# Products of the key/value stage on ScalarE, weight conversions behind the last scores, and other banks for `rp` and the first `vp`, in an attention and MoE kernel

## The chip, the cores and the metric

The kernel runs on one core of a Trainium2 chip. The metric is the device time of one execution in microseconds (us). A core has TensorE (PE, its weight load PEld), VectorE (DVE), ScalarE (ACT), GpSimd (POOL) and SyncE (SP, which here only issues DMAs). PSUM, the memory that TensorE writes, is handed out in banks; SBUF holds everything else on the chip.

## The reference, cut to what matters

```
a   = softmax(phi, over the 576 positions)            # phi (8, 8, 576, 32)
k_m = a^T k ;  v_m = a^T v                            # k, v (8, 8, 576, 64)
s   = softmax(q k_m^T / sqrt(64), over the 32 memories)
x   = (s v_m), heads side by side                     # (4608, 512)
xn  = x / sqrt(mean(x*x) + 1e-6) * rms_g
out = (silu(xn @ w_gate) * (xn @ w_val)) @ w_out      # 512 x 1536, 1536 x 512
```

The first two dimensions are batch (8) and head (8). [...] The wide products are made from high and low parts of each operand, three products for one, to keep the precision.

## The kernel before

**First stage** (pools `sb1`, `ps1`, `sbk`). Its batches come in pairs; pairs 0 and 1 go on to the second stage at once, 2 and 3 are finished there. For each batch `b`:
- `prep`: the load of `phi`, the maximum over positions (`mc`, VectorE L499), its transposition (`mt`, TensorE L506), the maximum (`mx` L514) and its spread (`mb` L518, VectorE; `mr` L523, TensorE), the subtraction from phi (VectorE L532), the exponentials into `e_bd` (ScalarE L542) and half sums `es` (GpSimd L554, L556).
- `kv_steps`: products `kvp` of the exponentials with k and v (TensorE L573), their sums in one more column (L588); in `post1` on VectorE `si` (the reciprocal of the sums), `im` (that with the mask of the head, L599), and `kb`, `vb` (the products scaled by `im`, L605); `turn` transposes them into `kvt` (TensorE L617), `post2` copies `km`, `vt` (ScalarE L627, L630) and scales `vg` by the rms gain (GpSimd L633), and `self_products` with `post3` make `gram`, from which the squares of x come.

For each pair and each of four head slots `s` stand the scores: `S` (TensorE L706), `mxs` and `ex` (VectorE L717, L719), the exponential (ScalarE L726), and in `norm` the sum, the addition of 1e-9 (L744), the reciprocal (L745) and the product `a` (GpSimd L746). Of each pair then come the `x_steps`: transposes `tp` of `a` (TensorE L184) with copies `at` (L194), the products `xp` (TensorE L235), squares `ssq` (VectorE L248), nine small steps and a loop of four Newton rounds on VectorE that end with `rinv`, 1/rms (`fin`, L259 to L276), the spread of `rinv` over the partitions `rp` (TensorE L204), `at` times `rp` (VectorE L212), and high and low copies `ath` (ScalarE L223) and `atl` (GpSimd L224). PSUM has tags `tr` (two banks, for transposes and `rp`), `kx` (two, for `kvp`, `kvt`, `xp`) and `S` (two tiles of two banks).

The **weights** are converted in blocks of 128x512 by `convert`. It starts with five VectorE steps on `raw`, the words that were loaded (`ex` L345, L347, L358; `mi` L365, L369), with two ScalarE steps between (L350, L376); then come the product `w` (L385, on VectorE or, by table `CE`, on GpSimd), the high part `wh` or `oh` (ScalarE L402) and the low part `wl` or `ol` (GpSimd L403). `ex`, `mi` and `w` have one buffer each for the gate and value weights of the first stage. `first_weights` is a list of steps: the loads of gate and value block 0, the conversion of gate block 0, a load, the conversion of value block 0, a load. `second_weights` goes on with blocks 1.

**Second stage** (pools `sb2`, `ps2`). For each slice of the hidden dimension: `vp`, the value vectors times the weights (`vw_steps`, TensorE L840, one buffer of two PSUM banks), copied as high part `xh` (ScalarE L853) and low part `xl` (VectorE L854) in two halves of 64 partitions; the gates and values `pg`, `pv` (`gv_steps`, L876); silu and product (L884, L885), high and low parts `hh`, `hl` (L898, L899), and the output products `po` (L918), added up in `acc` (L925).

**The order** of the first stage is not that of the code. Each step gets a due time, in us, from the table `PRM` (`CV` + i times `CP` for the i-th step of `first_weights`; `X_AT` for `x_steps`, `RO` for how long `spread` follows `fin`), the steps are recorded sorted by these times, and the framework then schedules what was recorded, by its own costs, into one row of instructions for each engine. `tc.issue_after(x)` keeps what is recorded under it behind instruction `x` in that order. With `reuse_waits="tile"` a tile waits for the earlier users of the memory or the bank that it gets:

```
        w = first_weights()
        ev += place(PRM["CV"], [PRM["CP"] * i for i in range(len(w))], w)
        ...
        for _, f in sorted(ev, key=lambda e: e[0]):
            f()
```

Of the kernel before, what the change touches and what calls it, by code (L numbers as in the profile page):

```python
# [40 lines left out]
    LAG=0.79,  # L41
    CV=114.79,
    CP=3.53,
    CV2=155.67,
# [7 lines left out]
    B=[2, 2, 2],  # L52
    RO=3.35,
    RS=4.63,
# [36 lines left out]
def kernel(  # L91
# [70 lines left out]

    def x_steps(pr, a, psum_t, psum_x, fetch=None):

# [34 lines left out]
        def spread(t0, n):  # L199

            def f():
                tps["r", t0] = tp = psum_t(f"rp{pr}_{t0}")
                for t in range(t0, t0 + n):
                    nc.tensor.transpose(  # L204
                        out=tp[:, (t - t0) * P:(t - t0 + 1) * P],
                        in_=rinv[pr][:, t:t + 1].broadcast_to([P, P]), identity=ident,
                    )
# [80 lines left out]
        for t0, n in ((0, 4), (4, 4), (8, 1)):  # L288
            events += zip((p + PRM["RO"], p + PRM["RO"] + PRM["RS"], p + PRM["RO"] + 2 * PRM["RS"]), spread(t0, n))
            p += PRM["RP"]  # L290
# [137 lines left out]
    with ExitStack() as c1:  # L428
# [133 lines left out]
        def kv_steps(b):  # L562
# [30 lines left out]
            def post1():  # L593
                kvp = st["kvp", b]
                si = sb.tile([P, 2, 1], F32, tag="si", name=f"si{b}")
                nc.vector.tensor_scalar_add(si, kvp[:, :, 128:129], 1e-9)
                nc.vector.reciprocal(si, si)
                im = sb.tile([P, 2, 2], F32, tag="im", name=f"im{b}")
                nc.vector.tensor_tensor(  # L599
                    out=im, in0=si.broadcast_to([P, 2, 2]),  # L600
                    in1=hmask.unsqueeze(1).broadcast_to([P, 2, 2]), op=ALU.mult,
                )
                st["kb", b] = [sb.tile([P, 2, 2, 64], F32, tag=f"{x}b", name=f"{x}b{b}") for x in "kv"]
                for i in range(2):
                    nc.vector.tensor_tensor(  # L605
                        out=st["kb", b][i],
                        in0=kvp[:, :, 64 * i:64 * i + 64].unsqueeze(2).broadcast_to([P, 2, 2, 64]),
                        in1=im.unsqueeze(3).broadcast_to([P, 2, 2, 64]),
                        op=ALU.mult,
                    )  # L610

            def turn():
                kb = st["kb", b]
                st["kvt", b] = tp = ps.tile([P, 2, HP, 64], F32, tag="kx", name=f"kvt{b}", bufs=PRM["B"][1])
                for i in range(2):
                    for cc in range(2):
                        nc.tensor.transpose(  # L617
                            out=tp[:, i, 2 * cc:2 * cc + 2, :].rearrange("p s m -> p (s m)"),
                            in_=kb[i][:, cc].rearrange("p h d -> p (h d)"), identity=ident,
                        )  # L620
# [77 lines left out]
        def score_steps(pr, s):  # L698
# [15 lines left out]
            def top():  # L714
                spv = st.pop(("sp", pr, s))[:, :NT * 64].rearrange("p (r m) -> p r m", m=M)
                mxs = sb.tile([P, R, 1], F32, tag="mxs", name=f"mxs{pr}_{s}")
                nc.vector.tensor_reduce(out=mxs, in_=spv, axis=AX.X, op=ALU.max)  # L717
                ex = sb.tile([P, R, M], F32, tag="ex", name=f"ex{pr}_{s}", bufs=2)
                nc.vector.tensor_tensor(  # L719
                    out=ex, in0=spv, in1=mxs.broadcast_to([P, R, M]), op=ALU.subtract  # L720
                )
                st["ex", pr, s] = ex
# [5 lines left out]
            def norm():  # L728
# [5 lines left out]
                else:  # L734
# [5 lines left out]
                    else:  # L740
                        for k in (8, 4, 2):
                            add(out=half[:, :, :k], in0=half[:, :, :k], in1=half[:, :, k:2 * k], op=ALU.add)
                        add(out=sm, in0=half[:, :, :1], in1=half[:, :, 1:2], op=ALU.add)
                nc.vector.tensor_scalar_add(sm, sm, 1e-9)  # L744
                nc.vector.reciprocal(sm, sm)  # L745
# [45 lines left out]
        for pr in range(G):  # L791
# [33 lines left out]
    def vw_steps(i):  # L825
# [20 lines left out]
        def evac():  # L846
            vp = vw[i][0]
            xh = sb.tile([P, 2, 2, 256], F32R, tag="xh", name=f"xh{i}", bufs=2)
            xl = sb.tile([P, 2, 2, 256], F32R, tag="xl", name=f"xl{i}", bufs=2)
            for h in range(2):  # L850
                rows = slice(64 * h, 64 * h + 64)
                src = vp[rows, :, ::-1, :] if h else vp[rows]
                nc.scalar.copy(xh[rows], src)  # L853
                nc.vector.tensor_tensor(out=xl[rows], in0=src, in1=xh[rows].bitcast(F32), op=ALU.subtract)  # L854
            vw[i] = xh, xl
# [165 lines left out]
    def x2(pr):  # L1021
        got = {}

        def fetch(t):
# [7 lines left out]
            return f  # L1032
        steps = x_steps(pr, got.pop, o_tile, o_tile, fetch)
        return [f for _, f in steps]
# [71 lines left out]
```

## Time and profile before

| | |
|---|---|
| three runs | 907.34, 907.63, 909.24 us; median 907.63 |
| the profiled execution | 910.09 us, span 908.3 us |
| mean granted TensorE clock | 0.969 |
| TensorE, VectorE, ScalarE, GpSimd busy | 838.9, 592.2, 421.1, 286.6 us |
| DMA | 106.41 MB, 117 GB/s |

The span runs from the first to the last instruction in the profile. TensorE's share differs by stage (us of busy time in each stretch, by the windows of the trace):

| stretch, us | TensorE | VectorE | ScalarE | GpSimd | granted clock |
|---|---|---|---|---|---|
| 0 to 40 | 26.3 | 21.0 | 15.6 | 16.1 | 0.87 |
| 40 to 80 | 36.5 | 27.9 | 24.2 | 20.3 | 0.87 |
| 80 to 120 | 27.6 | 37.9 | 20.0 | 25.7 | 0.83 |
| 120 to 160 | 25.0 | 30.3 | 15.5 | 17.3 | 0.82 |

The first stage ends near 157 us. In a row of the timeline stand the start, the length, engine, line, operation, the tile written and the tiles read without their numbers, the size and form, and in brackets how long the engine stood idle before it and what ended that.

### The profile page before, as it was taken

How to read it: one execution, taken by the hardware profiler on the slowest of the kernel's cores; microseconds unless marked ns; L12 is line 12 of the kernel's file. 1: busy time of each engine (PE TensorE's matmuls, PEld its weight loads, DVE VectorE, ACT ScalarE, POOL GpSimd, SP SyncE). 2: the span in 40 equal slices, each digit the busy share in tenths (PEclk: the TensorE clock that was granted, in tenths of full speed). 3: DMA queues.
4: the chain of work that ended last, by engine and by line, in shares of the span. 5: the costliest groups of instructions: out<-in, count | busy, mean ns of one | idle time of the engine just before them, and what ended most of it. 6: DMA issues, size and time to landing. Idle time of an engine off the chain costs nothing.

```text
span 908.3 us, 15828 instructions
## 1 busy us (share of the span) xinstructions
PE 838.9 (92%) x6207; PEld 744.3 (82%) x6207; DVE 592.2 (65%) x1026; ACT 421.1 (46%) x717; POOL 286.6 (32%) x242
## 2 busy tenths in 40 slices
PE   4989485899989999899999999999999999999997
PEld 3777474889887899788888997798889999999996
DVE  5577968997898877988754655632445455454543
ACT  2656433777766464665543343254424333243330
POOL 3463745333333324234242241412112121121120
PEclk9889887999999999999999999999999999999999
DMA  8976543553464341634214134411204012040046
GB/s 284 324 254 236 201 157 96 182 185 86 153 166 132 106 119 61 165 110 153 89 58 140 35 94 128 97 55 47 93 1 140 1 48 93 1 140 1 1 111 144
DMA packets 81506, 106.41 MB, mean 117 GB/s; under 512 B 34324, under 2 KB 52248, under 8 KB 81432
## 3 DMA queue, kind: packets, MB, share of 16 engines
q1 hardware_dynamic: 81432, 105.41, 37.6%
q8 instruction: 49, 0.80, 0.4%
q14 instruction: 25, 0.20, 0.1%
HBM read 73.93 MB, written 31.46 MB: 116 GB/s over the span
## 4 chain that ended last, share of the span: by engine, by line
PE 74%; DVE 14%; issue 4%; DMA 4%; ACT 3%; POOL 1%; SPq 0%; DVEq 0%; ACTq 0%; POOLq 0%
PE po L918 29%; PE pv L876 14%; PE pg L876 14%; PE vp L840 7%; PE kvp L573 3%; PE xp L235 1%; DVE mi L365 1%; DVE xl L854 1%; DVE ex L345 1%; DVE w L385 1%; ACT xh L853 1%; PE qtp L685 1%; DVE mi L369 1%; DVE acc L925 1%; DMA phi<-in_phi_dram 1%
## 5 line engine op out<-in xcount | busy, mean ns | idle before, releaser
L899 POOL TENSOR_TENSOR hl<-hf,hh 128x512 fp32r<-128x512 f32 (+1 forms) x96 | 139.6, 1454 | 410.9 <-ACT hh L898 399.6
L925 DVE TENSOR_TENSOR acc<-po,acc 128x512 f32<-128x512 f32 x180 | 123.1, 687 | 130.2 <-PE po L918 129.5
L918 PE MATMUL po<-oh,hh 128*128 128x512 f32 x432 | 173.6, 403 | 3.6 <-DVE acc L925 2.6
L918 PE MATMUL po<-oh,hl 128*128 128x512 f32 x432 | 171.1, 396 | 0.0
L918 PE MATMUL po<-ol,hh 128*128 128x512 f32 x432 | 170.9, 396 | 0.0
L884 ACT ACTIVATE sg<-pg 128x256 f32<-128x256 f32 x192 | 77.7, 409 | 163.2 <-PE pg L876 144.2
L854 DVE TENSOR_TENSOR xl<-vp,xh 64x1024 fp32r<-64x1024 f32 x96 | 117.2, 1220 | 45.9 <-ACT xh L853 44.4
L885 DVE TENSOR_TENSOR hf<-pv,sg 128x256 f32<-128x256 f32 x192 | 85.3, 453 | 73.0 <-PE pv L876 51.1
L853 ACT CAST xh<-vp 64x1024 fp32r<-64x1024 f32 x96 | 96.6, 1007 | 51.7 <-PE vp L840 21.6
L898 ACT CAST hh<-hf 128x512 fp32r<-128x512 f32 (+1 forms) x96 | 64.6, 673 | 82.3 <-DVE hf L885 57.0
L918 PEld LDWEIGHTS po<-oh,hl 128*128 128x128 f32 x432 | 81.5, 189 | 19.5
L918 PEld LDWEIGHTS po<-oh,hh 128*128 128x128 f32 x432 | 81.5, 189 | 19.3 <-DVE acc L925 4.5
L876 PE MATMUL pg<-ath,xh 128*128 128x320 f32 (+1 forms) x384 | 86.6, 299 | 7.9 <-ACT xh L853 6.3
L918 PEld LDWEIGHTS po<-ol,hh 128*128 128x128 f32 x432 | 81.7, 189 | 11.5 <-DMA ol<-od 0.2
L840 PE MATMUL vp<-wh,vm 128*128 128x256 f32 x384 | 85.5, 288 | 4.8 <-DVE at L212 2.3
L876 PE MATMUL pv<-ath,xh 128*128 128x320 f32 (+1 forms) x384 | 84.7, 300 | 4.7 <-DVE hf L885 4.6
L876 PE MATMUL pg<-ath,xl 128*128 128x320 f32 (+1 forms) x384 | 85.7, 296 | 0.0
L876 PE MATMUL pv<-atl,xh 128*128 128x320 f32 (+1 forms) x384 | 84.7, 296 | 0.0
L876 PE MATMUL pg<-atl,xh 128*128 128x320 f32 (+1 forms) x384 | 84.4, 297 | 0.0
L876 PE MATMUL pv<-ath,xl 128*128 128x320 f32 (+1 forms) x384 | 83.3, 296 | 0.0
L876 PEld LDWEIGHTS pg<-ath,xh 128*128 128x128 f32 x384 | 63.8, 190 | 13.3 <-ACT xh L853 6.6
L840 PEld LDWEIGHTS vp<-wh,vm 128*128 128x128 f32 x384 | 66.0, 191 | 8.4 <-DVE xl L854 3.0
(129 smaller groups left out, 1377.5 us busy)
## 6 DMA issues: line engine op xcount, KB each, us to landing
kv<-in_k_dram SPq DMA_DIRECT2D x32, 288.0 KB, 4.8
kv<-in_v_dram SPq DMA_DIRECT2D x32, 288.0 KB, 5.4
out_dram<-acc SPq DMA_DIRECT2D x72, 128.0 KB, 2.4
raw<-in_moe_w_gate_dram SPq DMA_DIRECT2D x12, 512.0 KB, 4.8
raw<-in_moe_w_val_dram SPq DMA_DIRECT2D x12, 512.0 KB, 3.7
wd<-wh SPq DMA_DIRECT2D x12, 512.0 KB, 3.0
wd<-wl SPq DMA_DIRECT2D x12, 512.0 KB, 4.1
raw<-in_moe_w_out_dram SPq DMA_DIRECT2D x12, 512.0 KB, 3.6
```

The lines of the kernel that those rows point to most:

```text
L235: nc.tensor.matmul(xp[64 * j:64 * j + 64, P * cc:P * cc + P], st["at"][:, t, cc, 64 * j:64 * j + 64], gb[:, j, cc], start=True, stop=True,)
L573: nc.tensor.matmul(kvp[64 * par:64 * par + 64, cc, 0:128], e_bd[j][:, hp, c, :], st["kv", b, hp][:, :, 64 * c:64 * c + 64], start=(c == 0) ...
L840: nc.tensor.matmul(vp[:, cc, e, :], lhs(l), r[:, 2 * cc + e, :], start=(n == 0), stop=(n == 2),)
L853: nc.scalar.copy(xh[rows], src)
L854: nc.vector.tensor_tensor(out=xl[rows], in0=src, in1=xh[rows].bitcast(F32), op=ALU.subtract)
L876: nc.tensor.matmul(pt[:, :N], l[:, cc, b, half * P:half * P + P], r[:, b, cc, t0:t0 + n, :].rearrange("p t x -> p (t x)"), start=(m == 0), ...
L884: nc.scalar.activation(sg[:, :N], pg[:, :N], AF.Silu)
L885: nc.vector.tensor_tensor(out=hf[:, :, b, :], in0=pv[:, :N].rearrange("p (t x) -> p t x", x=64), in1=sg[:, :N].rearrange("p (t x) -> p t x ...
L898: nc.scalar.copy(hh, hv)
L899: nc.gpsimd.tensor_tensor(out=hl, in0=hv, in1=hh.bitcast(F32), op=ALU.subtract)
L918: nc.tensor.matmul(po, l[:, tt, :], r, start=(m == 0), stop=(m == 5))
L925: nc.vector.tensor_tensor(out=accs[key], in0=po, in1=accs[key], op=ALU.add)
```

## The change

It has five parts. (1) `kb` and `vb` become one tile `kvb`, written by four ScalarE products, one for each half of the heads and each `cc`; `im` goes to GpSimd. (2) The addition of 1e-9 in `norm` goes from VectorE to GpSimd. (3) The steps of `first_weights` but the first load are recorded under `issue_after(st["less"])`, where `less` is the last score subtraction recorded by then, and their due times move from 114.79 + 3.53 i to 137.2 + 1.2 i. (4) `rp` of pair 0 takes a tile of tag `S`, with `RO` of pair 0 at 5.2 instead of 3.35; three empty tiles opened ahead of the second stage shift the PSUM banks that its first tiles get. (5) In `evac` both `xh` copies are written ahead of both `xl`.

```diff
-    CV=114.79,
-    CP=3.53,
+    CV=137.2,
+    CP=1.2,
...
-    RO=3.35,
+    RO=[5.2, 3.35],
...
-                tps["r", t0] = tp = psum_t(f"rp{pr}_{t0}")
+                tps["r", t0] = tp = psum_r(f"rp{pr}_{t0}")
...
                 im = sb.tile([P, 2, 2], F32, tag="im", name=f"im{b}")
-                nc.vector.tensor_tensor(
+                nc.gpsimd.tensor_tensor(
...
-                st["kb", b] = [sb.tile([P, 2, 2, 64], F32, tag=f"{x}b", name=f"{x}b{b}") for x in "kv"]
-                for i in range(2):
-                    nc.vector.tensor_tensor(
-                        out=st["kb", b][i],
-                        in0=kvp[:, :, 64 * i:64 * i + 64].unsqueeze(2).broadcast_to([P, 2, 2, 64]),
-                        in1=im.unsqueeze(3).broadcast_to([P, 2, 2, 64]),
-                        op=ALU.mult,
-                    )
+                st["kb", b] = kb = sb.tile([P, 2, 2, 2, 64], F32, tag="kvb", name=f"kvb{b}")
+                for cc in range(2):
+                    for h in range(2):
+                        nc.scalar.mul(
+                            kb[:, :, cc, h], kvp[:, cc, :128].rearrange("p (i d) -> p i d", i=2), im[:, cc, h:h + 1]
+                        )
...
-                nc.vector.tensor_tensor(
+                st["less"] = nc.vector.tensor_tensor(
                     out=ex, in0=spv, in1=mxs.broadcast_to([P, R, M]), op=ALU.subtract
-                )
+                ).ins
...
-                nc.vector.tensor_scalar_add(sm, sm, 1e-9)
+                nc.gpsimd.tensor_scalar_add(sm, sm, 1e-9)
...
-                    pr, lambda t, pr=pr: a_tiles[pr][:, t], tile_of("tr"), tile_of("kx"))]
+                    pr, lambda t, pr=pr: a_tiles[pr][:, t], tile_of("tr"), tile_of("kx"),
+                    tile_of("tr") if pr else lambda name: ps.tile([P, 1024], F32, tag="S", name=name, bufs=PRM["B"][2]))]
...
+        def behind(f):
+            def g():
+                with tc.issue_after(st["less"]):
+                    f()
+            return g
...
-        ev += place(PRM["CV"], [PRM["CP"] * i for i in range(len(w))], w)
+        ev += place(PRM["CV"], [PRM["CP"] * i for i in range(len(w))], [w[0]] + [behind(f) for f in w[1:]])
...
+    ps.tile([P, 512], F32, tag="o", name="o_first")
+    ps.tile([P, 512], F32, tag="v", name="v_first")
+    ps.tile([P, 2, 2, 256], F32, tag="vw", name="vw_first", bufs=1)
...
-            for h in range(2):
-                rows = slice(64 * h, 64 * h + 64)
-                src = vp[rows, :, ::-1, :] if h else vp[rows]
+            halves = [(slice(0, 64), vp[:64]), (slice(64, P), vp[64:, :, ::-1, :])]
+            for rows, src in halves:
                 nc.scalar.copy(xh[rows], src)
+            for rows, src in halves:
                 nc.vector.tensor_tensor(out=xl[rows], in0=src, in1=xh[rows].bitcast(F32), op=ALU.subtract)
```

Three places show what this makes of the rows of instructions. In the names the first number is the batch, the pair or the weight block and the last one counts tiles; lines of the changed kernel differ from the old ones by one up to `kvt`, by eleven at `xh`. The first is VectorE behind the maximum `mc` of batch 7, near the end of the first stage; before:

```order
L499 TENSOR_REDUCE mc7_0_1353<-phi7_1347 128x128
L745 RECIPROCAL sm1_2_1425<-sm1_2_1425 128x18
L605 TENSOR_TENSOR kb5_1318<-kvp5_1200,im5_1316 128x256
L605 TENSOR_TENSOR vb5_1319<-kvp5_1200,im5_1316 128x256
L744 TENSOR_SCALAR sm1_3_1472<-sm1_3_1472 128x18
L514 TENSOR_REDUCE mx7_0_1376<-mt7_0_1361 128x2
L212 TENSOR_TENSOR at0_900<-at0_900,rp0_8_1367 128x256
L745 RECIPROCAL sm1_3_1472<-sm1_3_1472 128x18
L345 TENSOR_SCALAR ex0_1_1709<-raw_01_1403 128x512
L365 TENSOR_SCALAR mi0_1_1714<-raw_01_1403 128x512
L518 COPY mb7_0_1378<-mx7_0_1376 128x128
```

And of the change, from the row behind `mc` and one step of a conversion:

```order
L366 TENSOR_SCALAR mi0_0_1379<-raw_00_1357 128x512
L744 RECIPROCAL sm1_3_1483<-sm1_3_1483 128x18
L348 TENSOR_SCALAR ex0_0_1369<-ex0_0_1369 128x512
L370 SCALAR_TENSOR_TENSOR mi0_0_1379<-raw_00_1357,mi0_0_1379 128x512
L359 SCALAR_TENSOR_TENSOR ex0_0_1369<-raw_00_1357,ex0_0_1369 128x512
L386 TENSOR_TENSOR w0_0_1390<-mi0_0_1379,ex0_0_1369 128x512
L346 TENSOR_SCALAR ex1_0_1423<-raw_10_1359 128x512
L366 TENSOR_SCALAR mi1_0_1462<-raw_10_1359 128x512
L515 TENSOR_REDUCE mx7_0_1364<-mt7_0_1351 128x2
L348 TENSOR_SCALAR ex1_0_1423<-ex1_0_1423 128x512
L370 SCALAR_TENSOR_TENSOR mi1_0_1462<-raw_10_1359,mi1_0_1462 128x512
L519 COPY mb7_0_1366<-mx7_0_1364 128x128
```

Gate and value blocks 0 (`ex0_0`, `ex1_0`) stood ahead of the last scores and now stand between `mc` and `mb` of batch 7; blocks 1 (`ex0_1`) went behind.

The second is TensorE behind the sums of batch 5, where `rp` of pair 0 stands; before:

```order
L204 MATMUL rp0_0_1256<-ident_58,rinv0_70 128x128 x4
L204 MATMUL rp0_4_1322<-ident_58,rinv0_70 128x128 x4
L506 MATMUL mt7_0_1361<-ident_58,mc7_0_1353 128x128
L204 MATMUL rp0_8_1367<-ident_58,rinv0_70 128x128
L617 MATMUL kvt5_1327<-ident_58,kb5_1318 128x128 x2
L617 MATMUL kvt5_1327<-ident_58,vb5_1319 128x128 x2
L573 MATMUL kvp6_1418<-kv6_0_1332,e_bd0_131 64x128
```

And of the change:

```order
L204 MATMUL rp0_0_1295<-ident_58,rinv0_70 128x128 x4
L204 MATMUL rp0_4_1341<-ident_58,rinv0_70 128x128 x4
L204 MATMUL rp0_8_1375<-ident_58,rinv0_70 128x128
L616 MATMUL kvt5_1314<-ident_58,kvb5_1309 128x128 x4
L574 MATMUL kvp6_1416<-kv6_0_1319,e_bd0_131 64x128
```

`mt` of batch 7 left its place ahead of `rp0_8` and `kvt5`; it now stands behind 13 rows of `kvp6`.

The third is ScalarE at the start of the second stage, around the first `xh`; before:

```order
L223 CAST ath1_1783<-at1_1503 128x2x64 x2
L350 ACTIVATE ex2_0_1828<-ex2_0_1828 128x512
L853 CAST xh0_1822<-vp0_1809 64x1024
L376 ACTIVATE mi2_0_1833<-mi2_0_1833 128x512
L853 CAST xh0_1822<-vp0_1809 64x1024
L402 CAST oh0_2027<-w2_0_1839 128x512
```

And of the change:

```order
L223 CAST ath1_1791<-at1_1510 128x2x64 x2
L650 COPY gram3_1750<-kvt7_1763 128x128
L351 ACTIVATE ex2_0_1839<-ex2_0_1839 128x512
L377 ACTIVATE mi2_0_1844<-mi2_0_1844 128x512
L403 CAST oh0_2038<-w2_0_1850 128x512
L864 CAST xh0_1833<-vp0_1820 64x1024 x2
```

The two `xh` copies now stand together, behind the high part `oh` of the first output weights.

More of the change, by code (lines that the diff above doesn't have):

```diff
@@ L618, in turn @@
                             out=tp[:, i, 2 * cc:2 * cc + 2, :].rearrange("p s m -> p (s m)"),
[L619 removed]
+                            in_=kb[:, i, cc].rearrange("p h d -> p (h d)"), identity=ident,
                         )
@@ L1032, in fetch @@
             return f
-        steps = x_steps(pr, got.pop, o_tile, o_tile, fetch)
+        steps = x_steps(pr, got.pop, o_tile, o_tile, o_tile, fetch)
         return [f for _, f in steps]
```

5 lines of the change are left out of this document (3 added, 2 removed).

## The prediction

> **What bounds the kernel now.** I read the page first, then the busy time by stage, then TensorE's row of instructions with the idle time before each, and then VectorE's, ScalarE's and GpSimd's rows around the gaps found there.
>
> ```profile
> span 908.3 us, 15828 instructions
> PE 838.9 (92%) x6207; PEld 744.3 (82%) x6207; DVE 592.2 (65%) x1026; ACT 421.1 (46%) x717; POOL 286.6 (32%) x242
> ```
>
> TensorE is busy for 92% of the span, but the average covers two stages with different limits:
>
> ```profile
> 80.00:120.00 40.00, 27.63 (x379) 22.98 (x380) 37.93 (x84) 20.01 (x39) 25.65 (x30) 0.83 0.45 152
> 120.00:160.00 40.00, 25.00 (x305) 22.11 (x302) 30.29 (x69) 15.49 (x29) 17.31 (x15) 0.82 0.48 146
> 700.00:750.00 50.00, 50.00 (x306) 45.37 (x306) 26.30 (x39) 17.15 (x28) 9.89 (x7) 1.00 0.11 38
> ```
>
> The columns are the length, then busy time of PE, PEld, DVE, ACT and POOL, the granted clock, and DMA. From 700 to 750 us TensorE has no gap: nothing that another engine does there is worth anything. From 80 to 120 us VectorE is busy for 37.93 of 40 us and TensorE for 27.63; from 120 to 160 us neither is full. These 80 us, the end of the first stage, are what the change can move. There TensorE's longer gaps are these (the start, the length, and in brackets the idle time with what ended it):
>
> ```profile
> 100.08 0.26 PE L588 MATMUL kvp<-ones,e_bd 128*64 128x1 f32 x2
> ...
> 105.99 1.94 PE L204 MATMUL rp<-ident,rinv 128*128 128x128 f32 x8 [5.66 <-DVE rinv L276]
> ...
> 112.97 0.45 PE L506 MATMUL mt<-ident,mc 128*128 128x128 f32 x1 [5.04 <-DVE mc L499]
> ...
> 143.25 1.09 PE L204 MATMUL rp<-ident,rinv 128*128 128x128 f32 x8 [1.97 <-DVE rinv L276]
> ...
> 148.31 0.39 PE L840 MATMUL vp<-wh,vm 128*128 128x256 f32 x1 [2.34 <-DVE at L212]
> ...
> 156.92 0.79 PE L876 MATMUL pg<-ath,xh 128*128 128x256 f32 x2 [6.32 <-ACT xh L853]
> ```
>
> They hold 21.3 us (5.66 + 5.04 + 1.97 + 2.34 + 6.32). The last is the door to the second stage: the first `pg` waits for the high copy `xh` of the first `vp`. What the change is worth is how much earlier that `pg` starts.
>
> **The change, part by part.** *First weight conversions behind the scores.* In the stretch before 105.68 us VectorE builds `rinv` of pair 0 between pieces of two conversions and the last scores:
>
> ```profile
> 86.15 0.17 DVE L744 TENSOR_SCALAR sm<-sm 128x18 f32<-128x18 f32 x1
> ...
> 91.70 1.66 POOL L554 TENSOR_TENSOR es<-e_bd 128x512 f32<-128x512 f32 x1
> ...
> 92.15 1.24 DVE L744 TENSOR_SCALAR sm<-sm 128x18 f32<-128x18 f32 x1
> ...
> 95.37 1.12 DVE L259 TENSOR_SCALAR m<-ssq 128x9 f32<-128x9 f32 x1
> 96.40 0.74 DVE L717 TENSOR_REDUCE mxs<-S 128x18 f32<-128x576 f32 x1
> ...
> 98.58 0.74 DVE L719 TENSOR_TENSOR ex<-S,mxs 128x576 f32<-128x576 f32 x1
> ...
> 105.68 0.16 DVE L276 SCALAR_TENSOR_TENSOR rinv<-u,rinv 128x9 f32<-128x9 f32 x1
> ...
> 138.88 0.17 DVE L259 TENSOR_SCALAR m<-ssq 128x9 f32<-128x9 f32 x1
> ...
> 143.02 0.17 DVE L276 SCALAR_TENSOR_TENSOR rinv<-u,rinv 128x9 f32<-128x9 f32 x1
> ```
>
> From the first `m` to the end of the last `rinv` it takes 105.84 - 95.37 = 10.5 us for pair 0. For pair 1, where no conversion stands between, it is 143.19 - 138.88 = 4.3 us. The changed kernel keeps one score pair in this chain (0.74 + 0.74), so 5.8 us: 4.7 us less. TensorE cannot use all of 5.66, since its own work ends at 100.34 and the VectorE row of the scaling then waits for a GpSimd sum of pair 1 (the addition of 1e-9 now stands there). I let `rp` of pair 0, and the `at` products behind it, start some 3.6 us before the 105.99 of `rp`, at 102.4.
>
> *The sum of batch 7's `mc` no longer precedes `kvt` on TensorE.* The gap of 5.04 goes, but what takes its place is late too: `kvt` now waits for four ScalarE products behind two `ath` casts. I estimate `kvp` of batch 6, which in the kernel before follows `mt` (112.97) and `kvt`, some 6 us earlier. But VectorE's `mc` waits for its transfer, so it ends only about 4 us earlier, at 108.8 against 110.72 + 2.10 = 112.8:
>
> ```profile
> 99.40 0.38 SPq L298 DMA_DIRECT2D phi<-in_phi_dram  x1
> phi<-in_phi_dram SPq DMA_DIRECT2D x7, 576.0 KB, 6.8
> 109.06 5.01 POOL L224 TENSOR_TENSOR atl<-at,ath 128x512 fp32r<-128x512 f32 x4 [0.72 <-ACT ath L223]
> ...
> 110.72 2.10 DVE L499 TENSOR_REDUCE mc<-phi 128x128 f32<-128x1152 f32 x1
> ...
> 113.20 0.40 DVE L605 TENSOR_TENSOR vb<-kvp,im 128x256 f32<-128x256 f32 x1
> ...
> 114.72 0.75 DVE L345 TENSOR_SCALAR ex<-raw 128x512 int32<-128x512 int32 x1
> ...
> 116.69 0.48 DVE L518 COPY mb<-mx 128x128 f32<-128x128 f32 x1
> ...
> 119.32 1.34 DVE L532 TENSOR_TENSOR phi<-phi,mr 128x1152 f32<-128x1152 f32 x1
> ...
> 119.60 1.28 POOL L385 TENSOR_TENSOR w<-mi,ex 128x512 f32<-128x512 f32 x1 [1.35 <-ACT mi L376]
> ...
> 130.55 0.43 DVE L345 TENSOR_SCALAR ex<-raw 128x512 int32<-128x512 int32 x1 [3.98 <-DMA raw<-in_moe_w_val_dram]
> ```
>
> Landing of phi: 99.40 + 6.8 = 106.2, then 2.1 for `mc` with two small steps ahead: 108.8.
>
> *Where the conversions go.* By the order of the changed kernel ten of their VectorE instructions now stand between `mc` and `mb` of batch 7, and `mb` feeds `mr`, the subtraction from phi, the exponentials and `tp` of pair 1. Their price: between 114.72 and 119.32 five such instructions and `mb` took 4.6 us beside GpSimd's `atl` (0.84 each without `mb`'s 0.4 us step). Ten are 8.4, with two small ones 8.9. So `mb` starts at 108.8 + 8.9 = 117.7, not at 116.69, and the subtraction, with 1.3 us for `mb`, the transpose and two handovers, at 119.0 against 119.32. All that was won up to here is spent again: -0.3 us. The bounds: 0.42 us for an instruction that meets no GpSimd work (the 0.43 of the row at 130.55) gives 4.7 instead of 8.9, thus -4.5; 1.25 us, a GpSimd step's length (5.01 / 4), for each of the ten gives 13.0, thus +3.8. I take 0.84 since GpSimd runs the same `atl` there.
>
> *Behind that.* The stall of 3.98 on a weight transfer goes: the load stands earlier in SP's queue against the key and value loads. In its place VectorE waits for GpSimd's product `w` of gate block 1, whose scratch tile it reuses: two `es` steps and the 1.28 of `w` begin only when the exponentials end, of which I count 1.0 us as uncovered, and ScalarE casts one `wh` (0.62) ahead of the exponentials. Squares that came one by one come later by 0.8: -3.98 + 1.0 + 0.6 + 0.8 = -1.6 at `kvp` of batch 7. There `xp` 8 is placed earlier among the key/value products, so that the `rinv` chain ends nearly with the sums: of the 1.97 idle before `rp` I take 1.3. The loads moved past the three kv loads of batch 6 on SP put batch 6's last kv load behind 1 MB of weights; it is needed about 109, and I price it at 0 (0 to 1.5).
>
> *Products on ScalarE.* They replace `im`, `kb` and `vb` on VectorE. The nearest rows are a copy of the same 128x128 size from PSUM and a GpSimd step on 18 columns:
>
> ```profile
> 84.77 0.22 POOL L743 TENSOR_TENSOR sm<-half 128x18 f32<-128x18 f32 x1
> ...
> 119.43 0.25 ACT L651 COPY gram<-kvt 128x128 f32<-128x128 f32 x1
> ```
>
> Four times 0.25 and 0.22 are 1.2 us of chain against two steps like the 0.40 of `vb` and a small `im`, about 1.0, on VectorE: nothing either way in the chain of a batch, and up to +1.5 in batches 1 and 3, where `im` stands in GpSimd's queue behind the `es` and `a` steps. I take 0 there, because TensorE does queued transposes meanwhile and the next key/value load, not `kvt`, sets batch 4. In batch 7 the pair `kb`, `vb` leaves the place between `rinv` (143.19) and `at` (143.97): -0.8.
>
> *The first vp on other banks, and high copies first.*
>
> ```profile
> 143.97 2.34 DVE L212 TENSOR_TENSOR at<-at,rp 128x1024 f32<-128x1024 f32 x2
> ...
> 153.76 0.94 DVE L358 SCALAR_TENSOR_TENSOR ex<-raw,ex 128x512 int32<-128x512 int32 x1
> 154.62 1.21 DVE L854 TENSOR_TENSOR xl<-vp,xh 64x1024 fp32r<-64x1024 f32 x1
> 155.75 0.67 DVE L385 TENSOR_TENSOR w<-mi,ex 128x512 f32<-128x512 f32 x1
> 155.86 1.01 ACT L853 CAST xh<-vp 64x1024 fp32r<-64x1024 f32 x1 [1.30 <-DVE xl L854]
> 156.89 0.62 ACT L402 CAST oh<-w 128x512 fp32r<-128x512 f32 x1
> ```
>
> The order lets `vp` go without its 2.34 wait, but ScalarE's queue now holds both `xh` copies behind the cast `oh` of the first output weights, which needs `w`. Both kernels pass through the same conversion, so the 2.34 buys nothing (bounds -2.3 and 0). After the end of `ex` at 154.6 stood `xl` and the second `xh`, to 156.87: 2.3 us. Now stand `w`, `oh` and two `xh`: 0.67 + 0.62 + 2.0 = 3.3. That is +1.0, and with the -0.8 above +0.2.
>
> In the loop behind, VectorE and ScalarE hand each other the halves:
>
> ```profile
> DVE xl L854 <- ACT xh L853: 44.4, 41, 4.0
> ACT xh L853 <- DVE xl L854: 20.6, 23, 1.7
> ```
>
> Both waits shrink, but TensorE, full there, waited for neither; 0, with bounds of 3 us either way for the order that shifts everywhere.
>
> Sum: -0.3 - 1.6 - 1.3 + 0.2 = -3.0 us. The profiled execution took 910.09 (its span plus 1.8) and would take 907.1; it lies 2.5 above the median of the runs, 907.63, from which I get 904.6.
>
> The Trainium skill, "SBUF — State Buffer", section on who interferes with whom, says that VectorE and GpSimd share one pair of ports under an exclusive lock, held for a whole instruction. The trace agrees: the 18-column addition at 92.15 took 1.24 us, not 0.17, and ended with the GpSimd step that ran from 91.70. The rule speaks against moving conversions beside `atl`; by it all ten could pay a full GpSimd step, which is the rival of +3.8 below.
>
> **The rivals.** (1) *The conversions run free and the early gain stays.* For it: the casts of `atl` also come earlier, and much of GpSimd's work may be over. Against: `atl`, `a` and `vg` follow in its queue up to about 114. At 0.42 each: -4.2 more, 900.4; with the waiting `vp` paid too, 898. (2) *Slower: each of the ten waits out a GpSimd step.* For it: the stretched rows above. Against: the same mix took 0.84. It gives 4.1 more than my sum, and with the waits of `im` behind `es` in batches 1 and 3 (up to 1.5 each) a further 3: 904.6 + 4.1 + 3 = 911.7. It decides from `mb` starting after about 121. (3) *No change.* The pieces cancel: GpSimd's `w`, the late weights or the kv load eat the 2.9 us of the third step: 907.5. For it: the first step already cancels by the sum. That the change doesn't do what it says can be for the banks only, and is in the sum with 0.
>
> **How the numbers follow.** A change under 0.2% (1.8 us) can hardly be told from none: 905.8 to 909.4. Chances: my sum 0.42, rival (1) 0.22, rival (3) 0.22, rival (2) 0.14. Faster takes (1) and nearly all of mine, 0.62; same takes (3) and the rest of mine, 0.23; slower 0.15. The predicted time is 904.6. The range is from 896.5 (below rival 1 by the loop's bound) to 909.5, which leaves out rival (2) and little else.
>
> **What would show it.** Right: `rp` of pair 0 about 4 us earlier with no long gap before it; `mb` of batch 7 near 117.7 with conversions ahead of it; no wait on a weight transfer near 126; `vp` right behind TensorE's last transposes and then a gap of 8 us up to a `pg` near 153.8. Wrong: conversion rows near 0.42 us or near 1.25 us in that stretch, a `kvt` that waits long for `im` in batches 1 to 4, or new gaps on TensorE after 200 us.

## The result, and the profile after

| | median, us | runs | ratio to the kernel before, 95% interval |
|---|---|---|---|
| before | 908.43 | 907.34 to 910.23 | |
| changed | 919.83 | 918.99 to 920.47 | 1.0123 [1.0103, 1.0143] |

The changed kernel is 11 us slower; 904.6 was predicted. Its page begins:

```profile
span 917.2 us, 15860 instructions
PE 844.1 (92%) x6207; PEld 746.1 (81%) x6207; DVE 584.3 (64%) x994; ACT 429.5 (47%) x749; POOL 292.6 (32%) x258
```

Busy time by stretch, columns as in the prediction, of the changed kernel and then, for the two middle stretches, of the kernel before:

```profile
80.00:120.00 40.00, 32.09 (x431) 25.72 (x431) 30.39 (x71) 20.61 (x45) 23.73 (x33) 0.91 0.41 136
120.00:160.00 40.00, 26.50 (x288) 22.72 (x289) 32.34 (x71) 20.59 (x42) 21.55 (x19) 0.78 0.63 197
200.00:300.00 100.00, 91.96 (x639) 81.32 (x639) 82.59 (x133) 66.24 (x110) 32.52 (x23) 0.98 0.42 127
300.00:500.00 200.00, 188.90 (x1281) 166.29 (x1280) 153.22 (x250) 103.07 (x173) 64.77 (x52) 0.99 0.35 111
700.00:750.00 50.00, 50.00 (x306) 45.38 (x305) 24.26 (x37) 17.29 (x28) 10.16 (x7) 1.00 0.14 45
```

```profile
200.00:300.00 100.00, 93.59 (x654) 82.36 (x653) 85.58 (x137) 69.10 (x116) 36.79 (x26) 1.00 0.47 138
300.00:500.00 200.00, 193.91 (x1334) 171.32 (x1333) 149.00 (x257) 103.84 (x176) 63.84 (x52) 1.00 0.36 109
```

VectorE lost 7.5 us between 80 and 120 us, as meant, and TensorE did more there. But TensorE loses 5.0 us between 300 and 500 us, where the change was expected to do nothing. Its longer gaps near the end of the first stage, in the changed kernel, behind the row in which `rp` of pair 0 starts:

```profile
103.29 0.65 PE L204 MATMUL rp<-ident,rinv 128*128 128x128 f32 x4
...
105.46 0.62 PE L204 MATMUL rp<-ident,rinv 128*128 128x128 f32 x4 [1.52 <-DVE si L597]
...
108.25 1.42 PE L616 MATMUL kvt<-ident,kvb 128*128 128x128 f32 x4 [1.37 <-ACT kvb L607]
...
120.65 0.33 PE L524 MATMUL mr<-ident,mb 128*128 128x128 f32 x1 [3.91 <-DVE mb L519]
...
142.85 1.09 PE L204 MATMUL rp<-ident,rinv 128*128 128x128 f32 x8 [1.13 <-DVE rinv L276]
...
146.53 0.45 PE L641 MATMUL kvt<-vt 128*64 128x64 f32 x8 [1.39 <-ACT vt L629]
...
156.89 0.79 PE L888 MATMUL pg<-ath,xh 128*128 128x256 f32 x2 [8.28 <-ACT xh L864]
```

`rp` of pair 0 starts 2.7 us earlier than before, without a gap ahead of it; 3.6 was forecast. But TensorE now waits 3.91 us for `mb` of batch 7, and the first `pg` starts at 156.89 us; before it was 156.92. In these two executions the first stage comes out even (a balance of gains and losses, as the experiments show), and the whole loss stands behind it: from the first `pg` to the end 917.2 - 156.9 = 760.3 us against 751.4. There the groups of instructions by line (busy us and mean ns, then the idle time before and its releasers) show TensorE waiting longer for `xl` and `sg`; the changed kernel, then the kernel before:

```profile
L888 PE MATMUL pg<-ath,xh 128*128 128x320 f32 (+1 forms) x384 | 87.1, 302 | 11.7 <-ACT xh L864 8.3 <-ACT sg L896 3.3
L852 PE MATMUL vp<-wh,vm 128*128 128x256 f32 x384 | 83.8, 288 | 5.9 <-DVE xl L866 5.7
```

```profile
L876 PE MATMUL pg<-ath,xh 128*128 128x320 f32 (+1 forms) x384 | 86.6, 299 | 7.9 <-ACT xh L853 6.3 <-ACT sg L884 1.5
L840 PE MATMUL vp<-wh,vm 128*128 128x256 f32 x384 | 85.5, 288 | 4.8 <-DVE at L212 2.3 <-DVE xl L854 2.3
```

### The profile page after: what moved, and what is told of

Same layout as the page of the kernel before. It is cut to its first block, busy times and chain, and to the rows that moved or that the text cites. A ratio compares the mean times of both kernels' runs of the same rounds, so it can differ in the third digit from the quotient of the medians.

```text
span 917.2 us, 15860 instructions
## 1 busy us (share of the span) xinstructions
PE 844.1 (92%) x6207; PEld 746.1 (81%) x6207; DVE 584.3 (64%) x994; ACT 429.5 (47%) x749; POOL 292.6 (32%) x258
## 4 chain that ended last, share of the span: by engine, by line
PE 67%; DVE 18%; ACT 5%; DMA 4%; issue 4%; POOL 1%; SPq 0%; DVEq 0%; ACTq 0%; POOLq 0%
PE po L930 27%; PE pv L888 13%; PE pg L888 13%; PE vp L852 6%; DVE xl L866 4%; DMA phi<-in_phi_dram 3%; DVE acc L937 2%; PE kvp L574 2%; DVE mi L366 2%; PE xp L235 2%; ACT xh L864 1%; DVE mi L370 1%; DVE ex L348 1%; DVE mc L500 1%; DVE ex L346 1%
## 5 line engine op out<-in xcount | busy, mean ns | idle before, releaser
L911 POOL TENSOR_TENSOR hl<-hf,hh 128x512 fp32r<-128x512 f32 (+1 forms) x96 | 141.9, 1478 | 416.8 <-ACT hh L910 342.1
L866 DVE TENSOR_TENSOR xl<-vp,xh 64x1024 fp32r<-64x1024 f32 x96 | 117.1, 1220 | 47.2 <-ACT xh L864 40.2
L897 DVE TENSOR_TENSOR hf<-pv,sg 128x256 f32<-128x256 f32 x192 | 83.2, 451 | 70.6 <-PE pv L888 51.2
L864 ACT CAST xh<-vp 64x1024 fp32r<-64x1024 f32 x96 | 96.7, 1008 | 45.8 <-PE vp L852 33.7
```

Source lines behind the costliest of these rows:

```text
L897: nc.vector.tensor_tensor(out=hf[:, :, b, :], in0=pv[:, :N].rearrange("p (t x) -> p t x", x=64), in1=sg[:, :N].rearrange("p (t x) -> p t x ...
L911: nc.gpsimd.tensor_tensor(out=hl, in0=hv, in1=hh.bitcast(F32), op=ALU.subtract)
```

## The experiments

Each run stands against the kernel before on the same chip. The chips differ, so two experiments are compared by their ratios. The last two columns are of one profiled execution each: the start of `rp` of pair 1, the last mark that all kernels share ahead of the second stage, and the time from there to the end.

| run | what | median, us | ratio, 95% interval | `rp` at | to the end |
|---|---|---|---|---|---|
| | before | | | 143.25 | 765.0 |
| | changed | 919.8 | 1.0123 [1.0103, 1.0143] | 142.85 | 774.4 |
| e1 | before, copies paired | 915.1 | 1.0062 [1.0046, 1.0078] | 142.49 | 771.1 |
| e2 | changed, copies unpaired | 916.2 | 1.0072 [1.0054, 1.0089] | 143.20 | 768.5 |
| e3 | before, conversions moved | 909.0 | 0.9994 [0.9977, 1.0011] | 141.68 | 765.0 |
| e4 | before, `kvb` on ScalarE, `im` on GpSimd | 922.1 | 1.0145 [1.0124, 1.0167] | 146.49 | 773.2 |
| e5 | e1, `vp` held behind `pv` | 928.3 | 1.0198 [1.0172, 1.0224] | 140.35 | 784.1 |
| e6 | before, slice 0 paired | 908.8 | 0.9993 [0.9979, 1.0007] | 140.97 | 765.1 |
| e7 | before, slices from 30 paired | 909.4 | 0.9990 [0.9971, 1.0009] | 143.04 | 765.5 |
| e8 | e4, `im` on VectorE | 917.4 | 1.0078 [1.0054, 1.0102] | 141.91 | 772.9 |
| e9 | paired, all else in the old order | 939.3 | 1.0332 [1.0309, 1.0354] | 143.23 | 791.6 |
| e10 | unpaired, in the order of e1 | 963.6 | 1.0594 [1.0562, 1.0627] | 140.00 | 818.2 |
| e11 | paired waits, old order throughout | 949.9 | 1.0445 [1.0420, 1.0470] | 143.31 | 806.4 |
| e12 | slice 0 paired, old order | 909.5 | 1.0002 [0.9986, 1.0018] | 137.84 | 768.0 |
| e13 | two tiles for each of `vp`, `xh`, `xl` | 920.5 | 1.0125 [1.0102, 1.0148] | 143.80 | 778.1 |
| e14 | e4, second stage in the old order | 914.6 | 1.0057 [1.0038, 1.0076] | 145.84 | 766.1 |
| e15 | e2, `kb`, `vb`, `im` back on VectorE | 911.3 | 1.0022 [1.0010, 1.0035] | 140.49 | 769.7 |
| e16 | e9, both `xl` at the later place | 935.5 | 1.0302 [1.0276, 1.0328] | 142.85 | 790.2 |
| e17 | e15, second stage in the old order | 907.4 | 0.9983 [0.9969, 0.9996] | 139.59 | 766.1 |
| e18 | e8, second stage in the old order | 910.1 | 1.0005 [0.9989, 1.0021] | 145.24 | 765.5 |

The start of `rp` is no exact measure: six kernels with the same first stage up to the copies of the first `vp` (before, e7, e9, e11, e12, e16) have it at 142.85 to 143.31 and once, in e12, at 137.84, where the time behind it is longer.

**One part at a time (e1 to e4).** e1 adds only the edit of `evac` to the kernel before; e2 takes only that edit out of the changed kernel; e3 adds only `CV`, `CP` and `issue_after`, which move the conversions (the steps that build float32 weights from pairs of 32-bit words); e4 only this:

```diff
-                nc.vector.tensor_tensor(
+                nc.gpsimd.tensor_tensor(
                     out=im, in0=si.broadcast_to([P, 2, 2]),
...
+                        nc.scalar.mul(
+                            kb[:, :, cc, h], kvp[:, cc, :128].rearrange("p (i d) -> p i d", i=2), im[:, cc, h:h + 1]
```

> The kernel before, with only the order of the copies of vp changed (both xh, then both xl). Theory A (the paired copies, and the order that the second stage gets with them, cost the whole loss): first pg near 157 us as before, then 9 to 12 us more than the kernel before, 917 to 920. Theory B (the loss comes from the first stage's moves, which make weights or queues late for the loop behind): 907 to 909, no change. By the prediction's own step (0, with 3 us either way): 905 to 911.

> The changed kernel with only the copies of vp put back (xh, xl, xh, xl); all else of the change stays. Theory A: 906 to 910, like the kernel before. Theory B: 917 to 920, like the changed kernel. The prediction's sum for the first stage alone would give 905.

> The kernel before, with only the first weight conversions moved behind the last scores (due times and issue_after). Its second stage keeps its order but for about 50 rows on TensorE. Theory A: 905 to 909; the rp of pair 0 comes about 4 us earlier, and the prediction's first steps say that what is won there is spent at mb of batch 7 and a wait on a weight transfer of 4 us goes. Theory B with this part as its cause: 913 or more.

> The kernel before, with only kb and vb on ScalarE and im on GpSimd. Theory A: no cost of its own in the first stage (the first pg within 1.5 us of 157), 905 to 911 in all, the spread because some 840 rows of the second stage on TensorE move. Theory B with this part as its cause (im waits behind es on GpSimd in batches 1 and 3, longer chain of a batch): first pg 2 us later or more, 911 or more.

Theory A had the larger half wrong: the pairing costs (e1), but the changed kernel without it is still 0.7% slower (e2), and the products on ScalarE with `im` on GpSimd alone cost about as much as the whole change (e4; the two intervals overlap). The conversions cost nothing and win nothing that can be measured (e3).

**Which copies, and does `vp` stand wrong (e5 to e7).** With paired copies the scheduler puts `vp` of slices 3 to 5 ahead of 12 products of the slice two before; in the kernel before it was 0 to 3. e5 forbids that; e6 and e7 pair some slices only:

```diff
-    VW=[-0.204, 0.03, 0.165],
+    VW=[-0.155, 0.03, 0.165],
...
+                key = (i - 2, 1, 1, 1)
+                with tc.issue_after(last_gv[key]) if key in last_gv else nullcontext():
+                    g()
```

> The kernel before with paired copies everywhere, as in the run that paired them alone, but vp of slice i is kept behind the last pv of slice i - 2 on TensorE (due time of its first half 0.05 of a slice later, and issue_after). Theory C (the pairing itself is no loss; the order it gets is: the scheduler takes the copies for quicker and puts vp ahead of pv, where it waits for the last xl): the first pg near 153, the stage behind it near 747 us instead of 756, in all 903 to 907. Theory D (each engine is held for two copies in a row, and sg, hf and acc come late): the stage behind stays near 756, in all 913 to 917. A strict order may cost by itself; between 907 and 913 both have a share.

> The kernel before with the copies paired for slice 0 alone. Theories C and D both: the first pg about 4 us earlier (153), as in the run that paired all. Behind it C: the rows of vp keep to where they stood in the kernel before (at most 6 of a slice's matmuls ahead or behind), so 747 to 749, in all 904 to 907; D: 747, too. A third theory, that any new order of the second stage costs 5 to 9 us by chance (as with the products on ScalarE alone), gives 751 or more behind the first pg, 909 to 914.

> The kernel before with the copies paired from slice 30 of 48 on, where TensorE had no gap of 0.15 us but one. C and D: no change, 907 to 910, since no engine but TensorE is full there. If pairing cost the engines time of its own that TensorE can't hide, some 18/48 of 9.5 us, 3.6 us more.

Theory C fell: with `vp` held the stage became slower still, its gaps now before `po` and `pg`. Pairing only the late slices costs nothing (e7), so the loss comes from the slices ahead. It is not bound to the stretch in which VectorE is fullest: against the kernel before, TensorE in the changed kernel is busy 1.7 us less from 160 to 300 us, where VectorE is busy for 89% of the time in the kernel before, and 5.9 us less from 300 to 600, where it is 69%. Pairing slice 0 brought the first `pg` closer to `rp` (11.6 us instead of 13.7), and none of it reached the end (e6), where theory C expected 904 to 907 us.

**Order and waits taken apart (e9 to e12).** Here all engines' instructions are held in a given order, by edges of issue order alone, added when everything is recorded (`order` is the scheduled order of the kernel named):

```diff
+        for n0, n1 in zip(order, order[1:]):
+            tc.add_manual_dep(
+                rows[engine][n1], rows[engine][n0].name,
+                mybir.DependencyInfo(mybir.DependencyClass.NoSync, mybir.DependencyReason.DATA), reason="order",
+            )
```

> The kernel before with paired copies everywhere, and every other instruction of every engine held in the order of the kernel before; only the second xh moves up behind the first, and the second xl behind the first. Theory E (the loss of the pairing alone, 9.5 us behind the first pg, is the new order that the scheduler makes of the second stage): first pg near 153, the stage behind it 744 to 749 us instead of 756, in all 902 to 907. Theory D (each engine held for two copies in a row, and the first xl waiting for both xh): the stage behind 754 or more, in all 912 or more.

> The counterpart: the copies in the code of the kernel before (the second xh waits for the first xl), but all engines held in the order that the run with paired copies alone had. Theory E: the stage behind the first pg takes 756 us or more (the order, and the waits between adjacent copies on top), in all 914 to 925. Theory D: both copies stand adjacent here too, so it is as slow; a stage behind the first pg under 752 would be against both.

> Paired copies in the code, but all engines in the order of the kernel before, the copies of vp too: only waits differ (the second xh no longer waits for the first xl, the first xl waits for both xh). Theory E: 747 us behind the first pg, within 2 us, in all 905 to 910. Theory D: also near 747 to 750, as nothing is adjacent; if the first xl's wait for the second xh is what costs, 753 or more.

> The kernel before, copies paired for slice 0 alone, every other instruction in the order of the kernel before. All theories: the first pg about 4 us earlier (153 instead of 157), and by theory E nothing of it lost behind: 746 to 748, in all 904 to 906. If the run that paired slice 0 alone lost its 4 us for another reason than the order (VectorE's and ScalarE's work is only put off at the start), 749 or more, 908.

Theory E fell for the copies: in the old order the pairing costs 30 us, not none (e9). The clearest run is e11: all four engines keep the kernel before's order, instruction for instruction, only the two waits differ, and it is 4.45% or 40 us slower. The reason can be seen in the rows of the copies. Before, ScalarE and VectorE take turns:

```profile
211.77 0.99 ACT L853 CAST xh<-vp 64x1024 fp32r<-64x1024 f32 x1
212.80 1.22 DVE L854 TENSOR_TENSOR xl<-vp,xh 64x1024 fp32r<-64x1024 f32 x1
214.06 1.01 ACT L853 CAST xh<-vp 64x1024 fp32r<-64x1024 f32 x1
215.10 1.23 DVE L854 TENSOR_TENSOR xl<-vp,xh 64x1024 fp32r<-64x1024 f32 x1 [0.75 <-ACT xh L853]
```

The second `xh` starts 0.04 us after the end of the first `xl`: the program makes it wait. In e1 the first `xl` waits for both `xh`:

```profile
216.82 2.03 ACT L852 CAST xh<-vp 64x1024 fp32r<-64x1024 f32 x2
218.88 2.46 DVE L854 TENSOR_TENSOR xl<-vp,xh 64x1024 fp32r<-64x1024 f32 x2 [3.19 <-ACT xh L852]
```

So the edit takes one wait away and puts another in its place: the four copies take 4.5 us one after another in either case (0.99 + 1.22 + 1.01 + 1.23 here, 2.03 + 2.46 there), and the wait moves from ScalarE to VectorE. In the old order that is where it hurts; waits between 160 and 600 us (sum, times, longest), before:

```profile
DVE xl L854 <- ACT xh L853: 12.7, 15, 4.0
PE po L918 <- DVE acc L925: 2.6, 3, 1.7
PE vp L840 <- DVE xl L854: 2.3, 3, 1.2
```

and in e9:

```profile
DVE xl L863 <- ACT xh L861: 29.4, 20, 5.0
PE po L927 <- DVE acc L934: 8.9, 7, 2.0
```

and in e11:

```profile
DVE xl L863 <- ACT xh L861: 62.0, 25, 5.0
```

ScalarE's wait for `xl`, 12.8 us there before, is gone in e11. Since e11 also keeps the copies where they were, with other work between the two of an engine, the first `xl` that waits for both `xh` is enough to cost time; theory D's other half, two copies in a row, is not needed.

e10 shows the reverse: the order of e1 is bad for the old waits, by 54 us, far more than was expected. Order and waits are fitted to each other, and the scheduler's own order for the paired copies gives back most of what the new wait costs (771.1 behind `rp` instead of 791.6), not all.

**Without the new wait (e13, e16).** e13 gives each half of the columns its own tiles, so that no copy waits for the other engine's other half; e16 is e9 with both `xl` moved to where the second stood. Of e13's edit, the line of `xh`; `vp` and `xl` are split likewise:

```diff
-            xh = sb.tile([P, 2, 2, 256], F32R, tag="xh", name=f"xh{i}", bufs=2)
+            xh = [sb.tile([P, 2, 256], F32R, tag=f"xh{c}", name=f"xh{i}_{c}", bufs=2) for c in range(2)]
...
```

> The kernel before with vp, xh and xl each as two tiles, one for each half of the columns (one PSUM bank each), copied in pieces of 64x512: neither engine's copy of one half waits for the other engine's copy of the other half. Theory F (the loss of the pairing is the wait that it puts in place of the one it takes away: the first xl, and VectorE's queue behind it, waits for both xh): with neither wait the stage behind rp of pair 1 takes 760 to 765 us (before 765.0, paired 771.1), in all 904 to 909, although each engine issues 96 copies more. Theory G (any order that the scheduler makes anew for the second stage costs some us, since the table of due times was made for the old one): 768 or more, 912 or more.

> As the run that paired the copies in the old order (939 us, 791.6 us behind rp of pair 1), but both xl stand where the second xl stood, not where the first did. VectorE then works on what stood between the two while ScalarE makes both xh. Theory H (what costs there is VectorE's queue held at the first xl, which now waits for both xh): most of the 26.6 us behind rp go, 765 to 775, in all 908 to 918. If the paired copies cost through what comes behind them (the next vp freed 1.2 us later by each last xl), 780 or more, 924 or more.

e13 cannot decide: its pieces cost VectorE 132.0 us instead of 117.2, and its second stage is ordered anew. e16 is clear: between 160 and 600 us VectorE no longer waits for `xh`, and TensorE waits for the later end of the copies instead:

```profile
PE vp L849 <- DVE xl L863: 14.5, 12, 3.6
```

Theory H fell as the only cause. The pair costs at the first place by holding VectorE and at the second by holding `vp`. The changed kernel has nearly the second stage of e1: from the first `pg` on, all but some 20 of TensorE's 4722 matmuls stand in the same sequence, and the time from there to the end is 760.3 us in one and 760.9 in the other. In both, TensorE waits longer than before for `xl` and for `sg`. So the loop loses what it loses in e1; how much of that is the wait and how much the new order was not settled. The changed kernel is 5.5 us slower than e1 (1.0123 less 1.0062), and its first `pg` starts 4.2 us later (156.89 against 152.69): most of that difference stands in the first stage.

**The products on ScalarE (e8, e14, e18) and the rest (e15, e17).** e8 and e18 put `im` back on VectorE; e14, e17 and e18 hold what the second stage records in the order of the kernel before.

> The kernel before with kb and vb on ScalarE, but im left on VectorE. If the wait of im in GpSimd's queue made the first stage late (161.5 instead of 156.9 for the first pg), the first pg comes at 157 to 158.5; if the four products on ScalarE did (370 ns each by the profile, 1.5 us a batch, and the wait for ScalarE's queue), at 160 or later. Behind the first pg its vp rows stand as in the run with im on GpSimd, so 753 us again, in all 911 to 920.

> kb and vb on ScalarE and im on GpSimd alone, as in the run of 922.1 us, but what the second stage records is held in the order of the kernel before. Theory G: from the first sg to the end 745 to 746 us as in the kernel before, not 750.6, in all 914 to 918; the rest of its loss stands before the first sg. If the 5.6 us behind the first sg were not the order's (late weights, or the clock), 750 again and 920 to 923.

> kb and vb on ScalarE with im left on VectorE, and the second stage held in the order of the kernel before. If of that part's loss the first stage's share is im in GpSimd's queue and the rest is the new order of the second stage, nothing is left: 907 to 911. If the four ScalarE products cost by themselves (370 ns each, behind what stands in ScalarE's queue): 912 to 915, like the run with im on GpSimd in the old order (914.6).

> The changed kernel with both parts put back that cost time by themselves: the copies of vp (xh, xl, xh, xl) and kb, vb, im on VectorE. Conversions behind the scores, the other banks and 1e-9 on GpSimd stay. If the losses add up, 906 to 910, like the kernel before; the prediction's sum for these parts (-0.3 - 1.6 - 1.3) gives 906.3. 912 or more would mean that these parts cost, too.

> The parts of the change that remain when the paired copies and the products on ScalarE are undone (conversions behind the scores, other banks, 1e-9 on GpSimd; 911.3 against 909.0 us for the kernel before), with the second stage held in the order of the kernel before. Theory G (the new order of the second stage made the 2 us): 906 to 909, and from rp of pair 1 to the end 765 us instead of 769.7. If the first stage's parts cost them: 911 again.

Three pairs differ in the order of the second stage alone: e4 and e14 (773.2 and 766.1 us behind `rp`), e8 and e18 (772.9 and 765.5), e15 and e17 (769.7 and 766.1). Theory G holds for these: the scheduler's new order, made because something earlier had moved, costs 4 to 7 us without a line of the second stage being touched. What is left of e14 (1.0057) goes when `im` returns to VectorE (e18, 1.0005): so the ScalarE products cost nothing that can be measured, and `im` on GpSimd costs some 4.5 us. e4 and e8, the same pair with the second stage ordered anew, lie 6 us apart (1.0145 and 1.0078). When `im` moves, the scheduler also orders the first stage anew; that share was not taken apart. In batch 1 of e14, a row of each of VectorE, GpSimd, GpSimd and ScalarE:

```profile
31.35 0.17 DVE L606 RECIPROCAL si<-si 128x2 f32<-128x2 f32 x1
```

```profile
32.66 1.26 POOL L565 TENSOR_TENSOR es<-es,e_bd 128x512 f32<-128x512 f32 x1
33.89 0.21 POOL L608 TENSOR_TENSOR im<-si,hmask 128x4 f32<-128x4 f32 x1
```

```profile
34.13 1.14 ACT L615 ACTIVATE kvb<-kvp,im 128x128 f32<-128x128 f32 x4 [0.17 <-POOL im L608]
```

and in e18 on VectorE:

```profile
32.92 0.17 DVE L606 RECIPROCAL si<-si 128x2 f32<-128x2 f32 x1
33.12 0.69 DVE L608 TENSOR_TENSOR im<-si,hmask 128x4 f32<-128x4 f32 x1
```

`im` needs 0.21 us but starts 2.37 us after `si`, behind `vg` and a sum `es` of GpSimd. The same stands in batches 3, 5 and 6 of e14 (2.44, 2.30 and 2.56 us); in e18, on VectorE, it is 0.03 us in batches 1, 3 and 6. In the changed kernel it is 1.58 and 2.21 us in batches 1 and 3 and at most 0.34 in the others. A delay comes with it: in the four kernels with `im` on GpSimd (changed, e2, e4, e14) `im` of batch 4 starts at 79.0 to 81.4 us, and the load of batch 7's `phi` is issued at 102.1 to 104.9; in the sixteen with it on VectorE these are 67.5 to 75.0 and 95.3 to 101.1. How the wait gets to batch 4 was not traced: TensorE has no gap of 0.5 us ahead of `kvt` in batches 1 to 4 of the changed kernel.

e17, the conversions, the other banks and 1e-9 on GpSimd with the second stage in its old order, is the only version whose interval lies below the kernel before: 907.4 us, 0.17% under it, and the interval nearly reaches 1.

## Why the prediction was wrong, step by step

- **The loop: the step that failed first.** "Both waits shrink, but TensorE, full there, waited for neither; 0, with bounds of 3 us either way for the order that shifts everywhere." "Full there" rests on 700 to 750 us. The prediction shows no window between 160 and 700 us; from 160 to 600 us the kernel before and then the changed kernel have (columns as above):

```profile
160.00:600.00 440.00, 420.26 (x2883) 372.20 (x2882) 332.45 (x575) 239.34 (x408) 147.13 (x113) 0.99 0.40 119
160.00:600.00 440.00, 412.61 (x2821) 364.45 (x2820) 335.31 (x568) 234.39 (x398) 147.10 (x112) 0.99 0.37 114
```

  There TensorE had 19.7 us of idle time (440 less 420.26) and now has 27.4, and VectorE is the fuller of the two engines that copy. ScalarE's wait for `xl` is gone, but VectorE's wait for `xh`, which now covers two copies instead of one, grew there from 12.7 to 19.2 us (over the whole span it shrank, from 44.4 to 40.2), and TensorE's wait for `xl` ahead of `vp` from 2.3 to 5.7:

```profile
DVE xl L866 <- ACT xh L864: 19.2, 7, 6.5
PE vp L852 <- DVE xl L866: 5.7, 6, 1.6
```

  So TensorE did wait, which the prediction ruled out. From the first `pg` to the end the time is 760.9 us in e1 and 760.3 in the changed kernel, against 751.4. The bound of 3 us for "the order that shifts everywhere" was too small by itself: e4 against e14 is 7 us.
- **`im` on GpSimd: a term taken as 0.** The prediction saw the wait ("up to +1.5 in batches 1 and 3") and priced it at 0, because "the next key/value load, not `kvt`, sets batch 4". The wait, 1.58 and 2.21 us, is not far above what it saw; the price was wrong. In all four kernels with `im` on GpSimd batch 4 comes later, and the move costs some 4.5 us at the end (e14 against e18; 1.0072 less 1.0022 in e2 and e15, with the products).
- **Conversions behind the scores: the first term was -0.3 and came out at +1.8.** In the changed kernel the ten steps took what was estimated, but they started late:

```profile
102.38 0.38 SPq L299 DMA_DIRECT2D phi<-in_phi_dram  x1
```

```profile
110.08 2.19 DVE L500 TENSOR_REDUCE mc<-phi 128x128 f32<-128x1152 f32 x1 [1.69 <-DMA phi<-in_phi_dram]
...
112.18 0.82 DVE L346 TENSOR_SCALAR ex<-raw 128x512 int32<-128x512 int32 x1
...
113.70 0.50 DVE L348 TENSOR_SCALAR ex<-ex 128x512 int32<-128x512 int32 x1
...
118.50 1.36 DVE L348 TENSOR_SCALAR ex<-ex 128x512 int32<-128x512 int32 x1
...
120.38 0.21 DVE L519 COPY mb<-mx 128x128 f32<-128x128 f32 x1
...
121.16 1.35 DVE L533 TENSOR_TENSOR phi<-phi,mr 128x1152 f32<-128x1152 f32 x1
```

  From the first step to `mb` it is 8.2 us, against 8.9 estimated. But `phi` landed near 110.0, not 106.2: its load was issued at 102.38 instead of 99.40, as late as in the other kernels with `im` on GpSimd. `mc` ended at 112.3 instead of 108.8, `mb` came at 120.4 instead of 117.7, and the subtraction from phi at 121.16 instead of 119.0 (before 119.32). Behind it the forecast was near: the stall on a weight transfer is gone, and from the subtraction to `rp` of pair 1 it is 2.2 us less than before (-1.6 and -1.3 were forecast), from there to the first `pg` 0.4 more (+0.2). With `im` left on VectorE these parts are worth between nothing that can be measured (e3) and -1.5 us (e17), not -3.2.
- **The door to the second stage.** "What the change is worth is how much earlier that `pg` starts" was too simple: in e6 and e12 it came 2.1 us earlier behind `rp`, and the end did not. In e12 the first `sg` starts 21.0 us behind `rp`, before 20.1: the casts of the output weights, which wait for VectorE's conversions, stand ahead of it on ScalarE.
- **The rivals.** The slower one gave 911.7, from two mechanisms. Its main one, ten steps that each wait out a GpSimd step (1.25 us), did not happen: they took 0.8 us on the mean. The Trainium skill ("SBUF — State Buffer", who interferes with whom) states that some kinds of VectorE instructions and those of GpSimd exclude each other from a shared pair of ports for a whole instruction. The trace agrees for single steps, but not each was stretched: `ex` at 118.50 took 1.36 us, while GpSimd's `wl` ran from 118.31 to 119.57; the same step at 113.70 took 0.50. The second mechanism, `im` behind `es`, did come. No rival had the paired copies. Of the prediction's own signs of being wrong, new gaps on TensorE after 200 us came; a `kvt` that waits long for `im` in batches 1 to 4 did not.

Taken back one after another, the parts are worth: the paired copies 4.6 us (1.0123 less 1.0072), the products on ScalarE with `im` on GpSimd 4.5 (1.0072 less 1.0022), the rest 2.0 (1.0022). By e17 the rest is -1.5 by itself, and 3.5 is the new order that the scheduler made of the second stage. These fill the 11.2 us by construction, each measured in the order that came with it; e14 and e18 find the same 4.5 us for `im` by another way.

## What to carry to other kernels

Reordering two engines' copies of one tile moves a wait rather than taking it away: ask which engine now waits, whether it is the fuller one, and what behind it the busiest engine needs. A tiny step on a critical chain belongs on the engine whose queue is short at that moment, not on the one with the least work in all. When a scheduler orders the whole program, compare an edit with the rest of the order held, because the new order alone can be worth several times the edit.

## What was not expected of the hardware

A ScalarE copy of 64x1024 takes 1008 ns and one of 64x512 takes 580; on VectorE 1220 and 687. Halving a copy thus adds some 150 ns on either engine, which is what made e13's pieces dear. And one of six executions of the same first stage was 5 us ahead of the others at the same instruction, so that a mark early in a single profile can't carry a verdict of a few us.
